# A planner that counts TensorE's changes of tiling mode and takes attention products in groups

## The chip, the cores and the metric

The kernel runs on one core of a Trainium2 chip. Its time is device microseconds of one execution; the median of three is 494.1 us (493.23 to 494.2). One more execution was profiled, and took 493.1 us. The engines are TensorE (PE in the profile, its weight loads PEld), VectorE (DVE), ScalarE (ACT), GpSimd (POOL) and SyncE (SP, which issues most DMAs).

## The reference

Linear attention with a decaying state, then a Fourier mixing over tokens and channels, a normalization and a feed-forward network (FFN), for 4 batches of 768 tokens, 8 heads of 48 and 384 channels:

```python
for t in range(S):
    state = alpha[:, :, t, :, None] * state + np.einsum('bhd,bhe->bhde', k[:, :, t], v[:, :, t])
    y[:, :, t] = np.einsum('bhd,bhde->bhe', q[:, :, t], state)
...
X = np.fft.fft(x, axis=1)
X = np.fft.fft(X, axis=2)
mixed = np.real(X).astype(np.float32)
u = x + mixed
mu = np.mean(u, axis=-1, keepdims=True)
var = np.mean((u - mu) ** 2, axis=-1, keepdims=True)
un = (u - mu) / np.sqrt(var + 1e-06)
ch = np.maximum(un @ w_ch1, 0.0) @ w_ch2
return (u + ch).astype(np.float32)
```

## The kernel before

**Work.** The recurrence is computed in chunks of 64 and 128 tokens. Two heads are handled together as a *pair* (4 pairs in a batch), one in rows 0 to 47, the other in rows 64 to 111. The stages of a pair (`attn_stages`, L750) are: scans of the decay on DVE (`s1` to `s3`), five transposes of keys (`s4`, tile `kt`), twelve *products* of keys and queries (`s5`: 48 rows deep, 128 x 128 out, copied by ACT to tiles of `w` or `x` and masked by POOL), ten *updates* (`s6`: keys times values, `vn`, 48 x 48 out into one PSUM tile) that DVE scales and chains to the states `tt`, and `s7`: for each half of the tokens 12 *values* (masked products times values, 64 columns wide) and 4 or 6 *state* matmuls (queries times `tt`, 112 rows, 64 columns) into one PSUM tile, which ACT copies to `y`. When the four pairs are done, *mixing* (`mix_stages`, L953) folds the sequence on DVE into `z` and takes 24 DFT matmuls with constants (`cst`) over tokens, then 12 over channels and two of one row; `norm_stages` (L1076) normalizes and takes nine transposes for each of the two token blocks, whose results are the FFN's input `x`. The FFN (`ffn_stages`, L1129) splits weights and inputs in a high and a low part: 432 matmuls a batch of 128 x 128 weights by 384 columns.

**PSUM.** Eight banks: three tiles `a` (attention, mixing and norms), two `f1` and three `f2` (FFN). Up to the first FFN matmul the attention may use all of them. The profile calls both of the FFN's `f`.

**Classes.** TensorE takes a matmul with over 64 rows and over 64 weight columns on the whole array (FFN, transposes, most of the DFT), one with at most 64 rows in a mode of short rows (products), one with at most 64 columns in a mode of narrow columns (updates, values, state); dummies and the one-row DFT matmuls have at most 32 columns, a mode of their own.

**Order.** Each operation is recorded with a key, and a `Plan` simulates all engines with estimated durations (`simulate`, L395). It writes the program in the order that this gives; all recorded operations therefore stand on L562 in the profile. Of the operations that an engine could start first, the one with the lowest key goes first. FFN matmuls (`fill`) of batch b have keys from b*1000+500, attention of batch b+1 from b*1000+420 (`KA`, `K1`), its mixing with the norm of the first token block b*1000+410 (`KM`), and the norm of batch b's own second block b*1000-595 (`KN`, so 405 for batch 1). So FFN work of one batch fills TensorE while attention and mixing of the next one come ready. The waiting rule (L460 to L464): right after an FFN matmul, operations that are ready, are no fill and have a key of 400 (`TOGETHER`) or more are kept back while fill is ready, until they sum up to 1.3 us (`ENOUGH`) or the first of them has waited 1.0 us (`PATIENCE`). Batch 0's attention has negative keys and runs alone, with dummies on `zero` (L1343 and L1345) put by count into TensorE's simulated gaps. `FX` lets the plan put some weight operations on DVE or POOL.

Of the kernel before, what the change touches and what calls it, by code (L numbers as in the profile page):

```python
# [33 lines left out]
GRP = 64  # L34
# [34 lines left out]
LONG = 3.0  # L69
FIRST = 2.8  # L70
NEAR = 3.0
TOGETHER = 400.0
ENOUGH = 1.3
PATIENCE = 1.0
LATE = 4.0
FAR = 12.0
SHORT = 20.0
# [120 lines left out]
class Plan:  # L198
# [39 lines left out]
    def add(self, engines, name, args, kwargs):  # L238
        engine = engines[0]
        fns = {e: self.method(e, name) for e in engines}  # L240
        if self.direct:
            return fns[engine](*[real(a) for a in args], **{k: real(x) for k, x in kwargs.items()})
        op = Op(engines, fns, args, kwargs, self.key)
        n = len(self.ops)
        self.ops.append(op)
        named = [("out" if i == 0 and "out" not in kwargs else i, a) for i, a in enumerate(args)] + list(kwargs.items())
        op.free, op.fill = 1, self.fill
        op.crit = CRIT[0] < self.key < CRIT[1] and not self.low
        op.bytes = None
        for k, a in named:  # L250
            if isinstance(a, Rows):
                a = a.view
            if isinstance(a, View):
                self.touch(n, op, a, k in ("out", "accum_out"))
                if k == "out":
                    op.free = self.region(a)[4]
                if k == 2:
                    op.moving = a
        op.name, op.loose = name, self.loose
        named = dict((str(k), a) for k, a in named)  # L260
        op.durs = {e: self.duration(op, named, e) for e in engines}
        op.port = self.port(op, named) if engine in ("DVE", "POOL") else None
        if engine == "SP" and isinstance(named["out"], View) and not self.loose:
            if self.chain is not None and self.chain not in op.deps:
                op.behind = self.chain
                op.deps.add(self.chain)
            self.chain = n
        if "dma" in name:
            op.wire = self.wire(named)

    def hold(self, view):

# [122 lines left out]
    def simulate(self, ghost=False, guess=None):  # L395
# [43 lines left out]
            due = coming[e][0][0] + shift if coming[e] else 1e9  # L439
            return t + op.durs[e] > due + HOLD[e] and t < due + GRACE  # L440

        placed, filled = 0, False
        while placed < len(ops):
            placed += 1
            best, spare = None, None
            for e, cand in wait.items():
# [11 lines left out]
                            continue  # L458
                    times.append((t, max(now, t), n))
                if e == "PE" and filled:  # L460
                    due = [x for x in times if x[0] <= now and not ops[x[2]].fill and ops[x[2]].key >= TOGETHER]
                    if due and any(x[0] <= now and ops[x[2]].fill for x in times):
                        if sum(ops[x[2]].durs[e] for x in due) < ENOUGH and now - min(x[0] for x in due) < PATIENCE:
                            times = [x for x in times if x not in due]  # L464
                if not times:
                    continue
# [1 line left out]
                for some, held_back in ((free, False), (times, True)):  # L468
                    if not some or (held_back and free):
                        continue  # L470
                    first = min(x[1] for x in some)
                    key, n, t = min((ops[n].key, n, max(t, now)) for t, late, n in some if late <= first + WINDOW[e])
                    if held_back:
                        if spare is None or t < spare[0]:
                            spare = (t, n, e)
                    elif best is None or t < best[0]:
                        best = (t, n, e)
# [7 lines left out]
            op.engine, op.dur = engine, op.durs[engine]  # L485
            if engine == "PE":
                filled = op.fill
            if guess and op.crit:
                for x in coming.values():
                    while x and done[x[0][1]]:  # L490
                        x.pop(0)
                shift = t - guess[n][0]
# [87 lines left out]
def gla_mix_ffn(ctx: ExitStack, tc: tile.TileContext, alpha, chunked, kq, pairkq, v, w1, w2, consts, rowtab, out):  # L580
# [169 lines left out]
    def attn_stages(b, hp, i, mixed, last):  # L750
# [115 lines left out]
                    G.affine_select(out=xs, in_=xs, pattern=[[0, 3], [1, P]], compare_op=ALU.is_ge, fill=0.0, base=0, channel_multiplier=-1)  # L866

        def s6():
            pu = psa()
            for a in range(NT - 1):  # L870
                for hd, r0 in enumerate((0, GRP)):
                    T.matmul(
                        pu[r0 : r0 + D, a * D : (a + 1) * D], e["kt"][:, a, r0 : r0 + D],
                        loaded["vn", pair][:, (2 * a + hd) * D : (2 * a + hd + 1) * D], start=True, stop=True,
                    )
            mt = e["mt"]
            for hd, r0 in enumerate((0, GRP)):
                r = slice(r0, r0 + D)
# [9 lines left out]
        def s7():  # L888
            X = e["X"]
            ytiles = mixed()[0]  # L890
            for h2 in range(2):
                py = psa()
                for c in range(3):
                    cc = 3 * h2 + c
                    cs = slice(cc * P, (cc + 1) * P)
# [7 lines left out]
                    if cc:  # L903
                        for lo in (0, GRP):
                            yo = py[lo : lo + GRP, o : o + 2 * GRP].rearrange("p (h e) -> p h e", h=2)[:, :, 0:D]
                            T.matmul(yo, e["A"][0:CW, cs.start + lo : cs.start + lo + GRP], tt[0:CW, cc - 1], start=False, stop=True)
                yo = py[:, 0 : 6 * GRP].rearrange("p (a h e) -> p a h e", a=3, h=2)[:, :, :, 0:D]
                FL["ev"].copy(ytiles[h2][:, :, hp * 2 * D : (hp + 1) * 2 * D].rearrange("p a (h e) -> p a h e", h=2), yo)

# [608 lines left out]
```

## Time and profile before

| | |
|---|---|
| median of three runs | 494.1 us |
| profiled execution | 493.1 us, span 491.4 us |
| granted TensorE clock | 0.999 of full speed |
| FFN matmuls | 1728, mean 341 to 342 ns to their modelled ends |
| values `a<-vn,w` | 576 records, mean 224 ns |
| state `a<-tt,w` | 288 records, mean 259 ns |
| products `a<-w,al` | 306 records, mean 289 ns |
| first FFN matmul | 70.47 us |

A group's duration in the table reaches to the modelled end of a matmul, and matmuls overlap; starts that follow each other tell the pace. The page names instructions by line, engine, operation, and out<-in without buffer numbers.

### The profile page before, as it was taken

What the parts mean: (1) busy time and instruction counts of PE and PEld (TensorE: products, weight loads), DVE (VectorE), ACT (ScalarE), POOL (GpSimd) and SP (SyncE); (2) the same over time, 40 slices, a digit from 0 to 9 for tenths busy, and PEclk for the clock granted to TensorE, in tenths of its full rate; (3) what the DMA queues carried; (4) which work ended last, traced back from release to release, by engine and by line L of the source; (5) the groups of instructions that cost most, each with busy time, mean ns of one, the idle gap of its engine ahead of it and who ended that gap; (6) DMA issues with size and microseconds to landing.
All of it is one profiled execution on the core that took longest, in us unless ns stands there. A gap on an engine that the chain in (4) does not pass through costs nothing.

```text
span 491.4 us, 10884 instructions
## 1 busy us (share of the span) xinstructions
PE 481.6 (98%) x4532; PEld 449.1 (91%) x4532; DVE 312.3 (64%) x693; ACT 182.9 (37%) x382; POOL 59.7 (12%) x86
## 2 busy tenths in 40 slices
PE   7999999999999999999999999999999999999995
PEld 6888989888889998888899999888999999999995
DVE  8878999886769997726599914736559314113112
ACT  3487487446762235443222314333112213111110
POOL 0321263101112000211020000122020000000000
PEclk9999999999999999999999999999999999999999
DMA  8869323327506022250140201110120001001001
GB/s 302 309 182 403 104 68 110 112 60 251 172 10 202 2 80 65 57 214 26 61 143 9 73 16 50 46 31 1 49 72 28 1 0 49 0 1 48 1 0 55
DMA packets 17687, 42.58 MB, mean 87 GB/s; under 512 B 2688, under 2 KB 8000, under 8 KB 17632
## 3 DMA queue, kind: packets, MB, share of 16 engines
q1 hardware_dynamic: 16576, 39.39, 23.8%
q0 software_dynamic: 768, 2.36, 1.8%
q8 instruction: 38, 0.62, 0.5%
q14 instruction: 17, 0.14, 0.1%
q10 hardware_dynamic: 288, 0.07, 0.1%
HBM read 31.97 MB, written 7.08 MB: 79 GB/s over the span
## 4 chain that ended last, share of the span: by engine, by line
PE 97%; DVE 2%; ACT 0%; ACTq 0%; issue 0%
PE f L562 67%; PE a L562 24%; PE a L1343 3%; PE f L1345 2%; PE f L1343 2%; DVE y L562 1%; DVE al L562 0%; ACT L562 0%; DVE st L562 0%; ACTq L562 0%; DVE x L562 0%; DVE mv L562 0%; ACT zero L562 0%; DVE w L562 0%; DVE back L562 0%
## 5 line engine op out<-in xcount | busy, mean ns | idle before, releaser
L562 PE MATMUL f<-x,wt 128*128 128x384 f32 x864 | 175.1, 342 | 0.7 <-ACT x L562 0.4
L562 PE MATMUL f<-wt,h 128*128 128x384 f32 x864 | 174.4, 341 | 0.0
L562 PEld LDWEIGHTS f<-x,wt 128*128 128x128 f32 x864 | 150.3, 188 | 3.4 <-DVE x L562 0.6
L562 PEld LDWEIGHTS f<-wt,h 128*128 128x128 f32 x864 | 149.7, 188 | 2.7 <-issue 0.2
L562 DVE SCALAR_TENSOR_TENSOR h<-f,h 128x384 fp32r<-128x384 f32 x96 | 53.2, 555 | 115.6 <-ACT h L234 115.0
L234 ACT ACTIVATE h<-f 128x384 fp32r<-128x384 f32 x96 | 47.1, 492 | 167.7 <-PE f L562 167.3
L562 POOL TENSOR_SCALAR_AFFINE_SELECT w<-w 128x384 f32<-128x384 f32 x48 | 25.2, 547 | 204.4 <-ACT w L562 204.4
L562 ACT COPY w<-a 128x384 f32<-128x384 f32 (+4 forms) x59 | 26.0, 482 | 41.9 <-PE a L562 41.9
L562 PE MATMUL a<-vn,w 128*64 128x64 f32 x576 | 27.4, 224 | 0.0
L562 DVE TENSOR_TENSOR tt<-a,w 48x240 f32<-48x240 f32 x30 | 12.1, 405 | 23.2 <-PE a L562 22.9
L562 PEld LDWEIGHTS a<-vn,w 128*64 128x64 f32 x576 | 23.6, 137 | 3.2 <-issue 3.0
L562 PE MATMUL a<-tt,w 112*64 112x96 f32 x288 | 26.3, 259 | 0.0
L562 DVE SCALAR_TENSOR_TENSOR y<-f,r,y 128x384 f32<-128x384 f32 x30 | 17.2, 613 | 13.7 <-PE f L562 13.7
L562 PEld LDWEIGHTS a<-w,al 48*128 48x128 f32 x306 | 19.7, 187 | 5.6 <-issue 4.3
L562 PE MATMUL a<-w,al 48*128 48x128 f32 x306 | 24.7, 289 | 0.0
L562 ACT COPY y<-a 128x288 f32<-128x288 f32 x29 | 11.6, 399 | 29.8 <-PE a L562 29.7
L562 DVE TENSOR_TENSOR y<-y,a 128x192 f32<-128x192 f32 (+6 forms) x66 | 20.6, 361 | 1.7 <-PE a L562 1.6
L562 DVE TENSOR_TENSOR_SCAN w<-al,d 128x768 f32<-128x768 f32 (+1 forms) x13 | 21.2, 1630 | 0.7 <-PE a L562 0.6
L562 DVE TENSOR_TENSOR_SCAN al<-al,back 128x768 f32<-128x768 f32 (+1 forms) x13 | 21.2, 1632 | 0.0
L562 DVE SCALAR_TENSOR_TENSOR tt<-tt,w 112x96 f32<-112x96 f32 x64 | 20.5, 321 | 1.0
L562 PEld LDWEIGHTS a<-tt,w 112*64 112x64 f32 x288 | 14.8, 136 | 6.0 <-issue 2.3
L562 DVE TENSOR_TENSOR z<-f 128x288 f32<-128x288 f32 (+3 forms) x40 | 19.7, 532 | 0.0
(128 smaller groups left out, 529.6 us busy)
## 6 DMA issues: line engine op xcount, KB each, us to landing
kq<-in_kq_dram SPq DMA_DIRECT2D x10, 768.0 KB, 6.7
wt<-in_w_dram SPq DMA_DIRECT2D x8, 768.0 KB, 6.0
out_dram<-y SPq DMA_DIRECT2D x24, 192.0 KB, 1.9
al<-in_chunked_dram SPq DMA_DIRECT2D x11, 392.0 KB, 4.7
vn<-in_v_dram SPq DMA_DIRECT2D x14, 296.0 KB, 4.1
wt<-in_w_dram SPq DMA_DIRECT2D x8, 384.0 KB, 6.2
scr<-y SPq DMA_DIRECT2D x4, 576.0 KB, 4.3
w<-w SPq DMA_DIRECT2D x28, 48.3 KB, 2.1
```

Of the source, the lines that this page charges most:

```text
L234: return lambda out, x: e.activation(out, x, AF.Relu)
L562: op.ins = op.fns[op.engine](*[real(a) for a in op.args], **{k: real(x) for k, x in op.kwargs.items()})
L1343: short = lambda *b: nc.tensor.matmul(bank(*b)[0:32, 480:512], zero.real(), zero.real(), start=True, stop=True)
L1345: long = lambda *b: nc.tensor.matmul(bank(*b)[0:32, 384:512], zero.real(), wide.real(), start=True, stop=True)
```

## The change

Two constants give a price to a change of mode in the plan: 0.09 us, and 0.19 us where the next operation is fill. Each recorded matmul gets a mode from its rows and columns (transposes count as mode 0). After an operation that is no fill, TensorE's candidates that can start no later than the first and have the same mode as the last one are taken first, if they are no fill, have a key of 400 or more and need no new tile. `together(n)` makes operations from number n on a group: the first gets the dependences on earlier operations and the tiles of all, the others depend on it. It is called for the ten updates of a pair and for each half's values and state, from batch 1 on. In the waiting rule, only operations whose key is at 420 or more in its thousand are kept back, so mixing (410) and the norms (410 and 405) are not; the two limits become tuples of equal values. No matmul, copy or DMA is added or taken away, but for the dummies.

```diff
+SWITCH = 0.09
+RETURN = 0.19
-ENOUGH = 1.3
-PATIENCE = 1.0
+ENOUGH = (1.3, 1.3, 1.3)
+PATIENCE = (1.0, 1.0, 1.0)
...
+        op.mode = 0
+        if engine == "PE" and name == "matmul":
+            (k0, k1), (m0, m1) = (self.region(dict(named)[x])[0:2] for x in (1, "out"))
+            op.mode = (1 if k1 - k0 <= GRP else 0) + (2 if m1 - m0 <= GRP else 0)
...
+    def together(self, n):
+
+        if not self.direct:
+            group = range(n, len(self.ops))
+            for m in group:
+                self.ops[n].deps |= {d for d in self.ops[m].deps if d < n}
+                if m > n:
+                    self.ops[m].deps.add(n)
+                for slot in self.ops[m].slots:
+                    if slot not in self.ops[n].slots:
+                        self.ops[n].slots.append(slot)
+                        slot.uses += 1
...
                 if e == "PE" and filled:
-                    due = [x for x in times if x[0] <= now and not ops[x[2]].fill and ops[x[2]].key >= TOGETHER]
+                    due = [x for x in times if x[0] <= now and not ops[x[2]].fill and ops[x[2]].key % 1000.0 >= KA and ops[x[2]].key >= TOGETHER]
                     if due and any(x[0] <= now and ops[x[2]].fill for x in times):
-                        if sum(ops[x[2]].durs[e] for x in due) < ENOUGH and now - min(x[0] for x in due) < PATIENCE:
+                        k = min(int(ops[x[2]].key // 1000) for x in due)
+                        if sum(ops[x[2]].durs[e] for x in due) < ENOUGH[k] and now - min(x[0] for x in due) < PATIENCE[k]:
...
                     first = min(x[1] for x in some)
+                    if e == "PE" and not filled:
+                        like = [x for x in some if x[1] <= first and ops[x[2]].mode == mode and not ops[x[2]].fill and ops[x[2]].key >= TOGETHER and all(s.cell is not None or not s.tag for s in ops[x[2]].slots)]
+                        some = like or some
...
             if engine == "PE":
                 filled = op.fill
+                if op.mode != mode:
+                    mode, op.dur = op.mode, op.dur + (RETURN if op.fill else SWITCH)
...
         def s6():
-            pu = psa()
+            pu, n = psa(), len(plan.ops)
...
+            if b:
+                plan.together(n)
...
-                py = psa()
+                py, n = psa(), len(plan.ops)
...
+                if b:
+                    plan.together(n)
```

TensorE, the values and state of batch 2's second pair (209.68 us before). `vn` are values, `w` with them a masked product, `tt` the state, `cst,al` a transpose of the next pair's keys. Before:

```order
L562 MATMUL a_379_2675<-vn_271_1982,w_3_367_2605 64x64 x8
L562 MATMUL a_379_2675<-tt_130,w_0_308_2236 64x2x48 x2
L562 MATMUL a_379_2675<-vn_271_1982,w_3_367_2605 64x64 x4
L562 MATMUL a_380_2693<-vn_271_1982,w_4_373_2641 64x64 x3
L562 MATMUL a_379_2675<-tt_130,w_0_308_2236 64x2x48 x2
L562 MATMUL a_380_2693<-vn_271_1982,w_4_373_2641 64x64
L562 MATMUL a_381_2701<-cst,al_275_1995 128x112
L562 MATMUL a_380_2693<-tt_130,w_0_308_2236 64x2x48 x2
L562 MATMUL a_380_2693<-vn_271_1982,w_4_373_2641 64x64 x4
L562 MATMUL a_381_2701<-cst,al_275_1995 128x112 x2
L562 MATMUL a_382_2712<-cst,al_275_1995 128x112 x2
L562 MATMUL a_380_2693<-tt_130,w_0_308_2236 64x2x48 x2
```

and of the change:

```order
L587 MATMUL f_1_336_2413<-wt_0_158_1181,h_377_2664 128x384
L587 MATMUL a_383_2704<-vn_271_1966,w_3_367_2600 64x64 x8
L587 MATMUL a_383_2704<-tt_130,w_0_318_2291 64x2x48 x2
L587 MATMUL a_383_2704<-vn_271_1966,w_3_367_2600 64x64 x4
L587 MATMUL a_383_2704<-tt_130,w_0_318_2291 64x2x48 x2
L587 MATMUL a_385_2724<-vn_271_1966,w_4_373_2627 64x64 x4
L587 MATMUL a_385_2724<-tt_130,w_0_318_2291 64x2x48 x2
L587 MATMUL a_385_2724<-vn_271_1966,w_4_373_2627 64x64 x4
L587 MATMUL a_385_2724<-tt_130,w_0_318_2291 64x2x48 x2
L587 MATMUL a_385_2724<-vn_271_1966,w_4_373_2627 64x64 x4
L587 MATMUL a_385_2724<-tt_130,w_0_318_2291 64x2x48 x2
```

The five transposes have moved ahead of an FFN run (they stand eight rows earlier), and each half's values are followed by their state without anything between.

TensorE, the change from the FFN of batch 0 to that of batch 1 (183.2 us before). `cst,f` and `cst,h` are the norms' transposes, `wt,h` FFN matmuls of batch 0, and those with `x_32` ahead of batch 1. Before:

```order
L562 MATMUL f_1_286_2101<-wt_0_273_1989,h_317_2295 128x384 x3
L562 MATMUL f_2_288_2108<-wt_0_273_1989,h_317_2295 128x384
L562 MATMUL a_323_2337<-cst,f_314_2276 128x128 x2
L562 MATMUL f_2_288_2108<-wt_0_273_1989,h_317_2295 128x384 x2
L562 MATMUL f_0_289_2113<-wt_0_273_1989,h_317_2295 128x384 x3
L562 MATMUL a_319_2304<-cst,f_314_2276 128x128
L562 MATMUL a_321_2312<-cst,f_314_2276 128x128
L562 MATMUL a_323_2337<-cst,f_314_2276 128x128
L562 MATMUL f_0_326_2360<-x_324_2354,wt_0_106_779 128x384 x2
L562 MATMUL f_1_328_2366<-x_324_2354,wt_0_106_779 128x384
L562 MATMUL f_0_326_2360<-x_325_2356,wt_0_106_779 128x384 x2
L562 MATMUL f_0_326_2360<-x_327_2362,wt_0_107_792 128x384 x2
```

and of the change:

```order
L587 MATMUL a_328_2355<-cst,h_325_2337 128x128
L587 MATMUL a_329_2357<-cst,h_325_2337 128x128
L587 MATMUL f_1_287_2102<-wt_0_270_1957,h_324_2330 128x384
L587 MATMUL a_327_2352<-cst,h_326_2347 128x128
L587 MATMUL a_328_2355<-cst,h_326_2347 128x128
L587 MATMUL a_329_2357<-cst,h_326_2347 128x128
L587 MATMUL f_2_289_2110<-wt_0_270_1957,h_324_2330 128x384
L587 MATMUL f_0_290_2114<-wt_0_270_1957,h_324_2330 128x384
L587 MATMUL f_0_331_2375<-x_319_2293,wt_0_104_736 128x384 x2
L587 MATMUL f_0_331_2375<-x_321_2303,wt_0_104_736 128x384 x2
L587 MATMUL f_0_331_2375<-x_322_2308,wt_0_108_790 128x384 x2
L587 MATMUL f_0_331_2375<-x_319_2293,wt_0_104_736 128x384
```

All 18 transposes of batch 1's norms now stand before its first FFN matmul, with FFN work of batch 0 between them; before, nine of them came behind it.

DVE, the start (11 us before). The operations on 768 elements of `w` with `d` and of `al` with `back` are the scans, `tt_129` the first pair's state. Before:

```order
L562 SCALAR_TENSOR_TENSOR w_2_3_68<-al_36_101,d_131 128x768
L562 RECIPROCAL back<-w_2_3_68 128x6
L562 RECIPROCAL rec<-w_2_3_68 128x6
L562 TENSOR_TENSOR w_2_3_68<-w_2_3_68 128x5
L562 TENSOR_TENSOR tt_129<-f_0_48_113,w_0_1_66 48x5x48 x2
L562 SCALAR_TENSOR_TENSOR al_36_101<-al_36_101,back 128x768
L562 SCALAR_TENSOR_TENSOR tt_129<-tt_129,w_0_1_66 112x96
L562 TENSOR_TENSOR w_2_3_68<-w_2_3_68,rec 128x6x64
L562 SCALAR_TENSOR_TENSOR tt_129<-tt_129,w_0_1_66 112x96
```

and of the change:

```order
L587 SCALAR_TENSOR_TENSOR w_2_3_68<-al_36_101,d_131 128x768
L587 RECIPROCAL back<-w_2_3_68 128x6
L587 RECIPROCAL rec<-w_2_3_68 128x6
L587 TENSOR_TENSOR w_2_3_68<-w_2_3_68 128x5
L587 SCALAR_TENSOR_TENSOR al_36_101<-al_36_101,back 128x768
L587 TENSOR_TENSOR tt_129<-f_0_48_113,w_0_1_66 48x5x48 x2
L587 TENSOR_TENSOR w_2_3_68<-w_2_3_68,rec 128x6x64
L587 SCALAR_TENSOR_TENSOR tt_129<-tt_129,w_0_1_66 112x96
L587 TENSOR_TENSOR al_36_101<-kq_40_105,al_36_101 128x768
```

The scan of `al_36` has moved ahead of the two products that wait for the first updates.

More of the change, by code (lines that the diff above doesn't have):

```diff
@@ L440, in blocks @@
             return t + op.durs[e] > due + HOLD[e] and t < due + GRACE
-        placed, filled = 0, False
+        placed, filled, mode = 0, False, 0
         while placed < len(ops):
```

## The prediction

> **What bounds the kernel now.** I read the page first, then the chain of waits, then the waits, and last the timeline of TensorE in narrow windows.
>
> ```profile
> span 491.4 us, 10884 instructions
> ...
> PE 481.6 (98%) x4532; PEld 449.1 (91%) x4532; DVE 312.3 (64%) x693; ACT 182.9 (37%) x382; POOL 59.7 (12%) x86
> ...
> PE 97%; DVE 2%; ACT 0%; ACTq 0%; issue 0%
> ```
>
> The profiled execution took 493.1 us, 1.7 us of it outside the span; the median of the three runs is 494.1 us, 1.0 us more. TensorE (PE) carries 97% of the chain that ended last. Its busy share alone would prove little, because ends of matmuls are modelled. What counts is how far the starts of successive matmuls lie apart.
>
> ```profile
> 146.72 19.75 PE f L562 x112
> 166.47 8.71 PE a L562 x68
> ```
>
> These rows of the chain (start, duration, what) show 112 FFN matmuls in a row in 19.75 us: **0.176 us each**, the pace with nothing in between. The timeline of TensorE in the second pair of batch 2 shows what happens around attention work; its columns are start, time to the modelled end, operation, names, shape of the weights, count of records. An FFN matmul and a transpose are one record each, every other matmul two.
>
> ```profile
> 188.30 1.15 PE L562 MATMUL a<-cst,h 128*128 128x128 f32 x9
> 189.20 1.30 PE L562 MATMUL f<-x,wt 128*128 128x384 f32 x6
> ...
> 204.69 1.49 PE L562 MATMUL f<-wt,h 128*128 128x384 f32 x7
> 206.02 0.69 PE L562 MATMUL f<-x,wt 128*128 128x384 f32 x3
> 206.63 0.94 PE L562 MATMUL a<-w,al 48*128 48x128 f32 x12
> 206.85 0.50 PE L562 MATMUL a<-w,al 48*128 48x128 f32 x6
> 206.96 0.50 PE L562 MATMUL a<-w,al 48*128 48x128 f32 x6
> 207.50 0.66 PE L562 MATMUL a<-vn,kt 128*48 128x48 f32 x20
> 207.85 0.30 PE L562 MATMUL a<-vn,kt 128*48 128x48 f32 x6
> 208.09 1.31 PE L562 MATMUL f<-x,wt 128*128 128x384 f32 x6
> 209.24 0.51 PE L562 MATMUL f<-wt,h 128*128 128x384 f32 x2
> 209.68 0.69 PE L562 MATMUL a<-vn,w 128*64 128x64 f32 x16
> 210.19 0.34 PE L562 MATMUL a<-tt,w 112*64 112x96 f32 x4
> 210.36 0.57 PE L562 MATMUL a<-vn,w 128*64 128x64 f32 x13
> ...
> 212.69 0.40 PE L562 MATMUL a<-vn,w 128*64 128x64 f32 x8
> 212.92 0.34 PE L562 MATMUL a<-tt,w 112*64 112x96 f32 x4
> 213.19 1.13 PE L562 MATMUL f<-wt,h 128*128 128x384 f32 x5
> ```
>
> (The rows of 206.85, 206.96 and 207.85 come from windows that begin inside a run.) Ten FFN matmuls between two attention pieces take 204.69 to 206.63, 1.94 us, where 10 x 0.176 is 1.76: 0.18 too much. Six products (48*128) take 0.87; inside the run they start 0.11 apart, so 0.66 was due: 0.21 too much. Ten updates (128*48) take 0.59; the first seven took 0.35, 0.05 each, so 0.50 was due: 0.09 too much. That round, FFN to products to updates to FFN, has three changes of the weights' shape class (full, short rows, narrow columns) and 0.48 us that no matmul explains: **0.16 us a change**.
>
> The stretch from 209.68 to 213.19 gives the price again: 24 values (0.23 us for four at 212.69, 0.058 each), ten state matmuls (0.17 for two at 210.19, 0.085 each) and five transposes (about 0.10, from 0.90 for nine at 188.30) make 1.39 + 0.85 + 0.50 = 2.74 us of the 3.51. Of the 0.77 left, the way in (0.51 at 209.68 for eight values, 0.05 over pace) and the way out (0.27 at 212.92 for two state matmuls, 0.10 over) take 0.15. Four changes between values, transposes and state take 0.62: again 0.16 each. Values and state have one class; between them the pace shows nothing.
>
> ```profile
> PEld a L562 <- issue: 11.1, 44, 0.3
> ```
>
> This row of the waits, TensorE's weight loads from 70.5 us to the last matmul, says it in another way: 44 times a load stood for about 0.25 us with no other engine to wait for.
>
> **The change, part by part.** *Fewer class changes.* Counted over the two built orders from the first FFN matmul on (70.47 us before) to the last one, consecutive matmuls change class 144 times before and 98 times after; by batch stage 49, 46, 45 and 4 before, 37, 29, 28 and 4 after. The work is the same: 1728 FFN, 192 products, 384 values, 160 state, 160 updates. Transposes stand amid values and state less often (25 changes before, 2 after), and FFN work no longer splits a half (from FFN to state 18 and none, from values to FFN 12 and none); the other kinds rise by 7. 46 x 0.16 = **7.4 us less**. Two changes from products to values and one from transposes to values are in no row of before; between products-to-updates and the dearest run above they cost 0.1 to 0.2 each, and I take 0.16. For the whole count the bounds are 46 x 0.09 = 4.1 (the least excess above) and 46 x 0.21 = 9.7 us; I take 0.16 since both stretches give it.
>
> *Groups.* The new dependences exist in the plan alone: on the chip a matmul waits for what it reads. But in TensorE's order a half's values now stand behind the state they are grouped with, and their evacuations behind them, then the mixing. What covers that delay is FFN work between the last attention matmul and the first mixing one: 112, 47 and 41 matmuls before, 102, 52 and 39 after in the three stages, at 0.176 still 18.0, 9.2 and 6.9 us. Without that cover a group's delay, at most the 3.5 us of the stretch above, would show. I cost it at nothing.
>
> *Mixing and norms exempt.* Their matmuls are of the full class, like the FFN's, so a piece alone costs no change. What it may move is the only place after 70.5 us where TensorE ran dry:
>
> ```profile
> 185.53 1.48 PE L562 MATMUL f<-x,wt 128*128 128x384 f32 x7 [0.36 <-ACT x L562]
> ...
> 187.32 1.14 PE L562 MATMUL f<-x,wt 128*128 128x384 f32 x5 [0.31 <-DVE x L562]
> ...
> 181.00:188.00 7.00, 6.33 (x38) 5.43 (x36) 6.96 (x17) 3.45 (x8) 0.00 (x0) 1.00 0.20 72
> ```
>
> The last row has busy time of PE, PEld, DVE and so on in 181 to 188 us: DVE is full (6.96 of 7.00) with additions and norms of batch 1, while TensorE has 0.67 us of nothing because the FFN of batch 0 has run out. Behind the last DFT matmul of batch 1, 17 FFN matmuls of batch 0 are left before and 61 after, 44 x 0.176 = 7.7 us more cover. I take **0.7 us less**; bounds 0 and, with the stretched FFN run at 185.53 (seven matmuls in 1.79 us, 0.56 over pace), 1.2.
>
> *The start, up to 70.5 us.* Class changes there hardly fall, 79 to 77, and are not what ends last.
>
> ```profile
> 0.00:70.50 70.50, 67.20 (x1108) 60.00 (x1108) 61.69 (x134) 42.17 (x83) 19.49 (x27) 1.00 0.64 226
> 70.50:150.00 79.50, 79.50 (x775) 71.48 (x774) 64.33 (x127) 47.91 (x92) 14.03 (x19) 1.00 0.41 131
> ...
> 14.13 0.82 DVE L562 TENSOR_TENSOR tt<-f,w 48x240 f32<-48x240 f32 x2 [1.31 <-PE f L562]
> 14.99 1.76 DVE L562 TENSOR_TENSOR_SCAN al<-al,back 128x768 f32<-128x768 f32 x1
> ...
> 46.51 9.74 PE L1345 MATMUL f<-zero 128*32 128x128 f32 x86
> 56.94 0.95 DVE L562 TENSOR_TENSOR wt<-wt,wt 128x768 fp32r<-128x768 f32 x1
> ```
>
> DVE works 61.69 of 70.50 us and mostly bounds; TensorE fills its gaps with dummies on zeros. In the new order DVE scans first and takes `tt` after it, so the 1.31 us wait at 12.8 is filled, and 36 long dummies stand where there were 43 (9.74/43 = 0.23 each, 1.6 us fewer). Against it, POOL hands one weight subtraction to DVE, 0.95 us by the last row. It comes behind the first FFN matmul's inputs, where DVE has 15 us free (64.33 of 79.50), and those hide it. I take **0.5 us less**, from bounds of 1.6 less and 0.95 more, nearer the middle as DVE's work ahead of the first FFN matmul is the same but for one operation of half a microsecond.
>
> *New waits.* Packed groups leave less room before an evacuation is needed: I add 0.5 us, about what TensorE lost at 181 to 188, from bounds of 0 and the slow rival below.
>
> **Sum.** -7.4 - 0.7 - 0.5 + 0.5 = -8.1 us. 493.1 - 8.1 = 485.0 for an execution like the profiled one, and 1.0 more for the median: **486.0 us**.
>
> **Rivals.** *A change is cheaper than its stretch.* If the excess is mostly weight loads that stay bare in a group as well, only 0.09 a change goes: 4.1 us and nothing else, 490.0. For it: at 208.09 eight FFN matmuls take 1.59 us, 0.18 too much, shared by two changes, so each FFN side is 0.09. Against it: both stretches sum to 0.16 when all sides are counted.
>
> ```profile
> L562 PEld LDWEIGHTS f<-wt,h 128*128 128x128 f32 x864 | 149.7, 188 | 2.7 <-issue 0.2
> ```
>
> Loads of 0.188 us fit a pace of 0.176, so inside a class a load hides beneath the matmul before it. The Trainium skill (TensorE: Matmul & The Clock Gate, Part 3, "What overlaps and what doesn't") holds that a load overlaps matmuls in flight only where its row group differs; FFN weights all use the full rows, so by that rule loads would be bare already and a change would cost just its drain, which is this rival's case. By that rule, the trace disagrees: a bare load alone would exceed the pace.
>
> *Evacuations set the pace: slower.* A half's values now stand together, and ACT must copy each PSUM tile out before one of the three tiles `a` comes free.
>
> ```profile
> L562 ACT COPY y<-a 128x288 f32<-128x288 f32 x29 | 11.6, 399 | 29.8 <-PE a L562 29.7
> ```
>
> A copy takes 0.40 us. There are 12 grouped pairs with three groups each. If each of the 36 stood bare by 0.23 us, the 8.1 us would be gone: no change. With the whole copy bare it is 36 x 0.40 = 14.4 us, and the time 494.1 - 8.1 + 14.4 = 500.4. For it: three tiles only. Against it: ACT waited 29.7 us for TensorE before these copies, not the reverse, and seven or more FFN matmuls (1.2 us) usually separate attention pieces. The Trainium skill (TensorEngine Tiling (Array Packing), "PSUM Bottleneck") warns that tiling speeds up TensorE but not the evacuation; no row of before shows TensorE waiting for one.
>
> *All bounds fall well.* 46 x 0.21 is 9.7 us, with 0.7 and half of 1.6 in the start 11.2: 483.
>
> *The plan does not do on the chip what it counts.* The saved changes are handed back where DVE is full (6.96 of 7.00 us): at most the gain of the first stage, 12 x 0.16 = 1.9 us, so this alone gives 488, inside the forecast's own spread of 484.5 to 488.5.
>
> **Chances.** Forecast 0.62; cheaper changes 0.14 (490.0); all bounds 0.12 (483); evacuations up to the 0.23 us point, no change, 0.05; beyond it 0.07 (about 500). The range takes in forecast and the two beside it: 482.5 to 491.0. Faster by over 0.2% (about what a measurement of this kernel can tell from no change) 0.88, within 0.2% 0.05, slower 0.07.
>
> **What would show it.** In the profile after, the row of loads waiting on "issue" should fall from 44 times to about 30; FFN matmuls should keep 0.176 us; values and state of a pair should run from start to end without a gap at 0.058 and 0.085 us; TensorE should have no idle time at the change from batch 0 to 1; the first FFN matmul should start near 70 us. Wrong it would be if `PE a <- ACT` waits appear (evacuations), if the excess in runs that remain grows over 0.16 us (the price was not per change), or if the first FFN matmul comes after 71.5 us.

## The result, and the profile after

The median is 486.05 us (485.96 to 486.44, four executions) against 493.67 us for the kernel before beside it: a ratio of **0.985, 95% interval [0.983, 0.987]**, 7.6 us less. The profiled execution took 485.96 us with a span of 484.3 us, 7.1 us less than before.

The page of the changed kernel: the span, the engines' busy time, and the shares of the chain that ended last.

```profile
span 484.3 us, 10874 instructions
...
PE 473.7 (98%) x4526; PEld 447.9 (92%) x4526; DVE 312.6 (65%) x695; ACT 181.2 (37%) x381; POOL 63.6 (13%) x85
...
PE 95%; ACT 1%; DMA 1%; SPq 0%; POOL 0%; DVE 0%; issue 0%; ACTq 0%
```

TensorE bounds it as before, and 98% busy tells as little as it did. Four views carry the reading. The first is the timeline of TensorE at the second pair of batch 2, the place where the prediction took its price (start, time to the modelled end, operation, weights, records).

```profile
207.95 0.65 PE L587 MATMUL a<-cst,al 112*128 112x112 f32 x5
208.36 1.82 PE L587 MATMUL f<-x,wt 128*128 128x384 f32 x9
210.03 0.33 PE L587 MATMUL f<-wt,h 128*128 128x384 f32 x1
210.29 0.69 PE L587 MATMUL a<-vn,w 128*64 128x64 f32 x16
...
212.40 0.34 PE L587 MATMUL a<-tt,w 112*64 112x96 f32 x4
212.67 0.96 PE L587 MATMUL f<-wt,h 128*128 128x384 f32 x4
```

The 24 values and ten state matmuls of the pair run from 210.29 to 212.67, 2.38 us, with nothing between them; before they took 3.51 us with five transposes among them. The transposes now stand between FFN matmuls and take 0.41 (207.95 to 208.36); the nine FFN matmuls behind them take 1.67, where 9 x 0.176 is 1.58, and that 0.09 is theirs too. So the five still cost 0.50, and 3.51 - 2.38 - 0.50 is 0.63 us saved here, 0.16 for each of four changes fewer. Next the pace, from the chain of work that ended last (start, duration, what):

```profile
143.61 18.04 PE f L587 x102
```

and the waits of TensorE's weight loads from 70 us to the end (us in total, times, longest):

```profile
PEld a L587 <- issue: 8.2, 32, 0.4
```

FFN keeps 0.177 us a matmul (18.04 / 102), and the row on "issue" fell from 44 times and 11.1 us to 32 and 8.2. The third view is a window at the change from batch 0 to batch 1 (busy time of PE, PEld, DVE, ACT and POOL):

```profile
181.00:188.00 7.00, 7.00 (x45) 6.92 (x44) 6.74 (x12) 4.06 (x9) 0.00 (x0) 1.00 0.26 80
```

and TensorE's timeline at its end, where the FFN of batch 1 begins:

```profile
184.26 0.49 PE L587 MATMUL a<-cst,h 128*128 128x128 f32 x3
184.51 0.60 PE L587 MATMUL f<-wt,h 128*128 128x384 f32 x2
184.94 3.34 PE L587 MATMUL f<-x,wt 128*128 128x384 f32 x18
```

TensorE no longer runs dry there (7.00 of 7.00, 6.33 before). The fourth view is the timeline again, of the first FFN matmuls of all; its first row is from before, where that run begins at 70.47:

```profile
73.83 1.77 PE L562 MATMUL f<-wt,h 128*128 128x384 f32 x9
...
68.99 3.43 PE L587 MATMUL f<-x,wt 128*128 128x384 f32 x18
72.58 1.14 PE L587 MATMUL f<-wt,h 128*128 128x384 f32 x5 [0.17 <-ACT h L236]
```

and ACT's at the same time:

```profile
70.56 1.28 ACT L587 ACT_TABLE_LOAD   x1
...
72.06 0.47 ACT L236 ACTIVATE h<-f 128x384 fp32r<-128x384 f32 x1
```

FFN begins at 68.99 instead of 70.47, 1.48 us earlier. Its first 18 matmuls take 3.59 us; before they took 3.36 (70.47 to 73.83). The first matmul on `h` waits 0.17 us for ACT, which loads a table for 1.28 us ahead of it. This small stall is new.

So far everything points one way. What doesn't is the length of the stages, from the first FFN matmul of a batch to that of the next (the last, to the last matmul):

| batch | 0 | 1 | 2 | 3 |
|---|---|---|---|---|
| before, us | 115.07 | 111.98 | 111.24 | 76.49 |
| after, us | 115.95 | 108.59 | 108.41 | 76.06 |
| class changes, cut at the same marks | 53 to 39 | 44 to 29 | 45 to 28 | unchanged |

Batches 1 and 2 fall by about 0.16 us a change (2.4 and 2.7 of 3.4 and 2.8). Batch 0's stage has 14 changes fewer, lost the first of the two dry places, and is 0.9 us *longer*. That 0.9 is the mark and not the kernel: by the trace's records the four stages held 18, 21, 18 and 6 transposes of the norms before and hold 27, 18, 18 and none after, so nine of them, 0.9 us at 0.10 each, were moved into this stage. (The six that left batch 3's stage are its 0.43 less, with a wait of 0.17 against them.) Like for like the stage is as long as before, where 14 changes (2.2) and the dry place (0.6) should have made it 2.8 us shorter. The products that run in it, those of batch 1, show why. First a usual set of six (two heads, three chunks; TensorE's timeline around 214 us), then one from batch 1, with ACT's copy of the transposes ahead of it:

```profile
214.25 0.94 PE L587 MATMUL a<-w,al 48*128 48x128 f32 x12
215.12 1.85 PE L587 MATMUL f<-x,wt 128*128 128x384 f32 x9
...
96.50 0.69 ACT L587 COPY kt<-a 128x336 f32<-128x336 f32 x2
99.25 0.34 PE L587 MATMUL a<-tt,w 112*64 112x96 f32 x4
99.51 0.93 PE L587 MATMUL a<-w,al 48*128 48x128 f32 x6
100.38 1.50 PE L587 MATMUL f<-x,wt 128*128 128x384 f32 x7
101.81 0.93 PE L587 MATMUL a<-w,al 48*128 48x128 f32 x6
102.67 0.62 PE L587 MATMUL f<-wt,h 128*128 128x384 f32 x2
```

Six products whose heads alternate take 0.87 us (214.25 to 215.12; two records each). In the lower rows three products of *one* head stand alone, FFN follows, then the other head's three: each trio takes 0.87 and 0.86 as well. Half the work takes the same time. By the trace's records, two to a product, a head's records stand 0.11 us apart in both cases, but for 0.21 behind the first; in the usual set the other head's stand 0.01 behind them (214.255 and 214.262), so both heads run side by side, and a trio runs alone.

It is so in three of batch 1's eight sets, because the plan gave the set one PSUM tile `a` at that point where it takes two. The transposes did not hold the other: ACT had copied them out 2.3 us before (at 97.19, by the row above), and 2.3 and 0.6 us before in the other two places. The kernel's text gives a reason that no run tests by itself: a tile is given out of the recorded order only while one more stays free (`KEEP`); the second half's values, recorded earlier and now a group that isn't ready, have not taken theirs; and the set's first product asks for two tiles at once, the other head's for one.

3 x 0.86 = 2.6 us: the 48 products of this stage took 6.95 us before and 9.52 now. Of neighbouring products on the same rows there are 12 after the change and 4 before, those in the start.

### The profile page after: what moved, and what is told of

It reads as the page before. It is cut to its first block, busy times and chain, and to the rows that moved or that the text cites. A ratio compares the mean times of both kernels' runs of the same rounds, so it can differ in the third digit from the quotient of the medians.

```text
span 484.3 us, 10874 instructions
## 1 busy us (share of the span) xinstructions
PE 473.7 (98%) x4526; PEld 447.9 (92%) x4526; DVE 312.6 (65%) x695; ACT 181.2 (37%) x381; POOL 63.6 (13%) x85
## 4 chain that ended last, share of the span: by engine, by line
PE 95%; ACT 1%; DMA 1%; SPq 0%; POOL 0%; DVE 0%; issue 0%; ACTq 0%
PE f L587 67%; PE a L587 24%; PE f L1374 2%; PE f L1372 1%; DMA al<-in_chunked_dram 1%; PE a L1372 1%; SPq L587 0%; ACT c L587 0%; POOL x L587 0%; DVE y L587 0%; ACT x L587 0%; ACT h L236 0%; ACT L587 0%; ACT f L587 0%; ACT kt L587 0%
## 5 line engine op out<-in xcount | busy, mean ns | idle before, releaser
L587 POOL TENSOR_SCALAR_AFFINE_SELECT w<-w 128x384 f32<-128x384 f32 x48 | 28.7, 619 | 196.8 <-ACT w L587 196.8
L587 PE MATMUL a<-w,al 48*128 48x128 f32 x306 | 27.6, 289 | 0.0
L587 PEld LDWEIGHTS a<-w,al 48*128 48x128 f32 x306 | 21.9, 187 | 5.8 <-issue 3.8
L587 PE MATMUL a<-tt,w 112*64 112x96 f32 x288 | 24.6, 248 | 0.0
L587 DVE SCALAR_TENSOR_TENSOR y<-f,r,y 128x384 f32<-128x384 f32 x30 | 17.1, 613 | 10.2 <-PE f L587 10.1
L587 POOL DMA_INDIRECT y<-scr,rows x12 | 14.6, 1213 | 55.4 <-DMA scr<-y 38.7
L587 DVE TENSOR_TENSOR y<-y,a 128x192 f32<-128x192 f32 (+5 forms) x66 | 20.7, 362 | 1.6 <-PE a L587 1.6
```

The costliest lines, as they stand in the source:

```text
L587: op.ins = op.fns[op.engine](*[real(a) for a in op.args], **{k: real(x) for k, x in op.kwargs.items()})
```

## Experiments

The change stands at 486.05 us; the kernel before, beside these runs, at 493.52 (first four), 493.17 (the next four), 493.22 and 493.15 (the last three). Intervals are those of the ratio to it. As it moves by 0.5 us from group to group, differences to the change of less than that say nothing.

**The groups taken out** (`e1_no_groups`): the price of a change against its rival.

```diff
-            if b:
-                plan.together(n)
...
-                if b:
-                    plan.together(n)
```

> The change without its groups (updates, values and state are planned one by one again); the price of a mode change, the preference for the same mode and the exemption stay. The built order has 133 class changes from the first FFN matmul on, against 98 with groups, and no two products on the same rows behind one another, against 12. Theory (each change costs 0.16 us, each product behind one on the same rows 0.11 us): 35 x 0.16 - 12 x 0.11 = 4.3 us more than the change, about 490.4 us. Rival (groups delay evacuations and cost what they save): no difference, 486 us. Rival (a change costs 0.09): 35 x 0.09 - 1.3 = 1.8 more, 487.9 us. The first FFN matmul starts at 69.0 us, as with groups.

Measured: 490.0 us, 0.994 [0.992, 0.996], 3.95 more than the change. The order has 133 changes instead of 98, and no two neighbouring products of one head. 35 x 0.16 = 5.6 less the 2.6 of the products is 3.0; with 0.09 a change it would be 0.6. The stages tell it more cleanly. Batches 1 and 2, with the same transposes and without a split set in either kernel, last 110.41 and 110.50 us against 108.59 and 108.41: 3.9 us for 25 changes, 0.156 each. Of the 0.9 us that isn't accounted for, 0.5 lies in batch 0's stage (115.52 against 115.95, where 10 changes more and no split set make 1.0 less), and 0.4 between medians and profiled executions (3.54 to the last matmul). The waits of TensorE's loads from 70 us on:

```profile
PEld a L587 <- issue: 8.1, 32, 0.3
PEld a L587 <- POOL w L587: 2.2, 9, 0.3
```

The "issue" row is the same as the changed kernel's, though this order has 35 changes more. The prediction wanted to read it as a count of changes. It counts ways from FFN into other work (36 for 36 lone probes below), and part of them stand under another releaser's name.

**Prices and preference for the same mode taken out** (`e2_no_mode`):

```diff
-SWITCH = 0.09
-RETURN = 0.19
+SWITCH = 0.0
+RETURN = 0.0
-                    if e == "PE" and not filled:
+                    if e == "PE" and False:
```

> The change without the price of a mode change and without the preference for the same mode; groups and exemption stay. The order has 106 class changes from the first FFN matmul on (98), 12 products on the same rows (12), and 43 long dummies in the start as before (36). Theory: 8 x 0.16 = 1.3 us for changes, and if the price is what moved the start, the first FFN matmul is back at 70.5 us and that adds 1.5 us: 488.8 us. Rival (the start moved for another reason, such as the groups): first FFN matmul at 69.0 and 487.3 us.

Measured: 487.72 us, 0.989 [0.987, 0.991], 1.7 more than the change. The order has 106 changes (8 x 0.16 = 1.3), and 43 long dummies stand in the start again; the first FFN matmul is at 70.14, 1.15 later, and doesn't meet the table load. The two make 2.4, more than came, so what the prices do through the count of dummies in the start counts about as much as the changes they save. The theory's 488.8 was too high, the rival's 487.3 nearer.

**The waiting rule as before** (`e3_mix_waits`): mixing and norms kept back again.

```diff
-... and ops[x[2]].key % 1000.0 >= KA and ops[x[2]].key >= TOGETHER]
+... and ops[x[2]].key >= TOGETHER]
-                        k = min(int(ops[x[2]].key // 1000) for x in due)
+                        k = min(2, min(int(ops[x[2]].key // 1000) for x in due))
```

> The change with mixing and norms kept back by the waiting rule again; price, preference and groups stay. The order has 102 class changes from the first FFN matmul on (98) and 16 products on the same rows (12). Theory: 4 x 0.16 + 4 x 0.11 = 1.1 us more, 487.1 us, and TensorE has gaps again between the FFN of batch 0 and that of batch 1 (0.7 us): 487.8 us. Rival (the exemption does nothing that counts): 486 us, no gaps there.

Measured: 487.3 us, 0.988 [0.987, 0.990], 1.25 more than the change. The theory's number is met, its reason hardly: the dry places do not come back. TensorE's timeline there:

```profile
186.59 1.15 PE L587 MATMUL a<-cst,h 128*128 128x128 f32 x9
...
188.25 0.51 PE L587 MATMUL a<-cst,al 112*128 112x112 f32 x3 [0.16 <-DVE x L587]
```

There is one wait of 0.16 us. The rest fits 102 changes (4 x 0.16 = 0.6) and 16 same-row neighbours instead of 12, which is one more split set (0.86). In `e1_no_groups` and `e2_no_mode` TensorE is busy through 181 to 190 us too, so the place stays full whichever of the three parts is left out, and which of them fills it stays open.

**Products as a group** (`e4_pairs`): the split sets repaired. From batch 1 on, a set's products form a group, and a pair's first transpose takes its target `kt` before it starts, so that it can't sit on PSUM.

```diff
                 for a in range(a0, a1):
                     T.transpose(...)
+                    if a == 0 and b:
+                        plan.hold(kt)
...
-                pc = [psa() for _ in range(2)]
+                pc, n = [psa() for _ in range(2)], len(plan.ops)
...
+                if b:
+                    plan.together(n)
```

> The change with the six products of a half as a group too, and the transposes of a pair taking their place in PSUM only when the tile that they are copied to is free. The order has 93 class changes from the first FFN matmul on (98), and no products on the same rows behind one another (12). Theory: 5 x 0.16 + 12 x 0.11 = 2.1 us less than the change, and the split runs of three products are gone: 483.7 us. Rival (products of one head are slow for their distance from other work, not for their rows, or the groups now delay the copies): 486 us or more.

Measured: **483.56 us**, 0.981 [0.979, 0.983], 2.5 less than the change. Batch 0's stage is 112.99 us long (115.95 in the change), and the set that was split at 99.51 takes what the others take, 106.98 to 107.85:

```profile
106.98 0.94 PE L587 MATMUL a<-w,al 48*128 48x128 f32 x12
107.85 1.31 PE L587 MATMUL f<-wt,h 128*128 128x384 f32 x6
```

There are no same-row neighbours left and 93 changes; the first FFN matmul is at 69.34, 0.35 later. 2.6 + 0.8 - 0.35 = 3.05 were due by that count, 2.5 came (2.59 to the last matmul). The two edits were not run apart.

**All sets with one head after the other** (`e5_same_rows`): the suspected cost, doubled and more, on the changed kernel.

```diff
-                for c in range(3):
-                    cs = slice(...)
-                    for hd, r in ((0, slice(0, D)), (1, slice(GRP, CW))):
+                for hd, r in ((0, slice(0, D)), (1, slice(GRP, CW))):
+                    for c in range(3):
+                        cs = slice(...)
```

> The change with the six products of a half in another order: three of one head, then three of the other, in place of one of each in turn. The same work; the order has 124 products behind one on the same rows against 12, 104 class changes from the first FFN matmul on against 98. Theory (a product behind one on the same rows starts 0.22 us after it, on the other rows 0.11 us): 96 such products behind the first FFN matmul are 84 more than now, 84 x 0.11 + 6 x 0.16 = 10.2 us more, 496 us, and inside a run of three the starts lie 0.22 us apart everywhere. Rival (the runs of three were slow because each was cut off by FFN work, so two class changes fell on three products): 487 us, starts 0.11 us apart.

Measured: 494.43 us (ten executions), 1.003 [1.001, 1.004], 8.4 more than the change. A change of two loops that adds no instruction gives back all that the change gained. The size was expected at 10.2; six in a run cost less than two trios:

```profile
92.62 1.26 PE L587 MATMUL a<-w,al 48*128 48x128 f32 x12
93.81 0.66 PE L587 MATMUL a<-vn,kt 128*48 128x48 f32 x20
```

1.19 us for six in this order, 0.87 alternating, 0.86 for three alone. By the trace's records the first head's run from 92.62 to 93.28 and the second's from 92.95 to 93.61, in each the products 0.33 and then 0.22 apart, as in a trio. So "0.22 apart on the same rows" held. What the sum lacked is that the second head starts 0.33 us behind the first and runs beside it: four same-row neighbours in a set cost 0.32 us, not 4 x 0.11.

**The price by itself** (`p1_spread`, `p2_bunch`, `p3_full`): 36 probes, small matmuls of 32 columns of zeros with a weight tile of 64 columns, in the last 216 FFN matmuls of batch 3, where nothing else runs. In `p1_spread` each stands alone, which makes 170 changes in the program; in `p2_bunch` they stand at one place, 100 changes; `p3_full` is `p1_spread` with weights of 128 columns, FFN's class, 98 changes.

```diff
+    def probe(times):
+        if "to" not in probing:
+            probing["to"] = psa()
+        for _ in range(times):
+            T.matmul(probing["to"][0:GRP, 0:32], ident[:, 0:GRP], zero, start=True, stop=True)
+            plan.ops[-1].deps.add(len(plan.ops) - 2)
...
# p2_bunch: if f == f0: probe(36)
# p3_full: T.matmul(probing["to"][:, 0:32], ident, zero, start=True, stop=True)
```

> The change with 36 extra matmuls of narrow columns (64 weight columns, 32 moving columns, on zeros) in the last 216 FFN matmuls, one ahead of each three that finish a token block, so that each stands alone: 72 class changes more, 170. Their results are not used. Theory: against the kernel with 36 extra matmuls on the whole array at the same places, 72 x 0.16 = 11.5 us more. Rival (0.09 us a change): 6.5 us. Rival (0.20 us, as the plan's two constants of 0.09 and 0.19 make 0.14 each): 10.1 us for 0.14.

> The change with the same 36 narrow matmuls all at one place of the last FFN: 2 class changes more, 100. Theory: they cost their pace alone, about 0.05 us each, 1.8 us, and 0.3 us for two changes: 488.2 us. The kernel with them spread is then 70 x 0.16 = 11.2 us slower than this one. Rival (a narrow matmul is itself dear, changes are not): this one costs as much as the spread one.

> The change with 36 extra matmuls on the whole array (128 weight columns, 32 moving columns, on zeros) at the places of the spread narrow ones: no class change more, 98. Theory: about 0.1 us each for a load of 128 columns and a short matmul, 3.6 us: 489.7 us, and FFN matmuls beside them keep 0.176 us. Rival (any foreign matmul amid FFN work breaks its pace, whatever its class): as much as the spread narrow ones, 497 us or more.

Measured: 502.09 us, 1.018 [1.016, 1.021]; 490.42, 0.994 [0.992, 0.996]; 493.94 (ten executions), 1.0015 [1.000, 1.003]. TensorE's timeline of `p1_spread`:

```profile
455.33 0.30 PE L587 MATMUL a<-zero,cst 128*64 128x32 f32 x2
455.56 0.80 PE L587 MATMUL f<-wt,h 128*128 128x384 f32 x3
456.29 0.30 PE L587 MATMUL a<-zero,cst 128*64 128x32 f32 x2
```

of `p2_bunch`:

```profile
445.62 4.38 PE L587 MATMUL a<-zero,cst 128*64 128x32 f32 x72
449.93 2.38 PE L587 MATMUL f<-wt,h 128*128 128x384 f32 x12
```

and of `p3_full`:

```profile
452.69 0.30 PE L587 MATMUL a<-zero,cst 128*128 128x32 f32 x2
452.83 0.77 PE L587 MATMUL f<-wt,h 128*128 128x384 f32 x3
453.44 0.30 PE L587 MATMUL a<-zero,cst 128*128 128x32 f32 x2
```

A probe in the bunch takes 4.31 / 36 = 0.12 us. A round of one probe alone and three FFN matmuls takes 0.96 (455.33 to 456.29), less 0.12 and 3 x 0.176 that is 0.31 for two changes. The two medians give 11.67 / 70 = **0.167 us a change**, the two spans (499.8 and 489.4) 0.15. That is the mean price, by work that shares nothing with attention.

Against `p3_full` 11.5 us were expected and 8.15 came. The third probe was meant to show a probe without a change, and is poorer at that: its round is 0.75, so a probe takes 0.22, not the expected 0.1 and 0.10 more than one of the bunch. With that 36 x 0.10 put back it is 11.75 us, 0.163 for each of 72 changes. Is the 0.22 a price for standing alone among FFN matmuls? Hardly, by an estimate: a transpose, one record with weights of the same 128 columns, takes 0.10 in a run (0.90 for nine at 188.30 before), so a probe of two records would take 0.20 anyway. No run puts 36 of these at one place.

The probes also show what the row on "issue" counts (`p1_spread` from 400 us on), one wait for each probe, though each makes two changes:

```profile
PEld a L587 <- issue: 9.0, 36, 0.3
```

**Dearer changes in the plan** (`e6_price`, on `e4_pairs`): both prices at 0.2, `SWITCH = 0.2` and `RETURN = 0.2`.

> The kernel with the products grouped, and the plan's two prices set to 0.2 us each (0.09 and 0.19). The order has 92 class changes from the first FFN matmul on (93), 18 short dummies fewer in the start, no products on the same rows. Theory (0.16 us a change, the start set by DVE): 0.2 us less than the kernel with the products grouped, 483.4 us. Rival (the start follows the dummies): up to 18 x 0.06 = 1.1 us less, 482.5 us.

Measured: ten executions that scatter, five from 485.82 to 486.34 us, the profiled one 486.01 among them, four from 487.89 to 496.23, and one of 1576.32, which no run explains; the median of all is 487.11, the ratio 0.988 [0.985, 0.991]. The five lie 2.4 us above `e4_pairs`; 483.4 was expected, and missed. Behind the start it is like `e4_pairs`; the loss lies ahead of it, as TensorE's timeline shows (the last number is idle time and what ended it):

```profile
62.42 0.98 PE L587 MATMUL a<-cst,x 96*128 96x192 f32 x4 [0.41 <-DVE y L587]
...
71.55 0.61 PE L587 MATMUL f<-x,wt 128*128 128x384 f32 x2
```

The first FFN matmul comes 2.2 us later than in `e4_pairs`. The DFT begins 0.57 of it later (55.18 against 54.61); behind it TensorE waits for DVE's `y` three times, 0.91 us in all, and dummies fill more. A price in the plan moves batch 0's order as well, where there is hardly a change to save.

**Seven long dummies more** (`e7_dummies`, on the change): does DVE set the start, or do the dummies?

```diff
-... * int((t - t0) / DUMMY[kind]))
+... * (int((t - t0) / DUMMY[kind]) + 7 * (kind == 1)))
```

> The change with seven more long dummies ahead of the DFT of batch 0, 43 as before the change; nothing else differs. Theory (the dummies stand in front of the first DFT matmul, which has its input by then): the DFT starts 7 x 0.22 = 1.5 us later, the first FFN matmul at 70.5 us instead of 69.0, 487.5 us. Rival (DVE's work ahead of the first FFN matmul, 1.1 us earlier than before, sets the start): the first FFN matmul stays at 69.0 to 69.5 us, 486.0 to 486.5 us.

Measured: 487.74 us, 0.990 [0.988, 0.992], 1.7 more than the change, as expected. TensorE's timeline:

```profile
46.11 9.74 PE L1374 MATMUL f<-zero 128*32 128x128 f32 x86
55.78 3.89 PE L587 MATMUL f<-cst,z 128*97 128x65 f32 x36
...
70.42 0.79 PE L587 MATMUL f<-x,wt 128*128 128x384 f32 x3
```

The DFT follows its dummies at once, and FFN begins at 70.42, as in the kernel before: seven matmuls on zeros held up the first FFN matmul.

**Five long dummies fewer** (`e8_fewer`, on `e4_pairs`): the same line with `- 5 * (kind == 1)`. Is there more to be had?

> The kernel with the products grouped, and five long dummies fewer ahead of the DFT of batch 0 (31 in place of 36); nothing else differs. Theory (the dummies still stand in front of the first DFT matmul): it starts 5 x 0.22 = 1.1 us earlier or as soon as DVE has its input, and the time falls by 0.5 to 1.1 us, 482.5 to 483.1 us. Rival (its input from DVE comes last by now): no difference, 483.6 us, with TensorE idle ahead of the first DFT matmul.

Measured: 483.2 us, 0.980 [0.978, 0.981], not clearly different from the 0.981 [0.979, 0.983] of `e4_pairs`. TensorE's timeline:

```profile
46.70 7.07 PE L1378 MATMUL f<-zero 128*32 128x128 f32 x62
54.55 3.86 PE L587 MATMUL f<-cst,z 128*97 128x65 f32 x36 [0.78 <-PE f L1378]
```

and DVE's:

```profile
53.58 2.87 DVE L587 TENSOR_TENSOR z<-f 128x6 int32<-128x6 int32 x5
```

TensorE is idle for 0.78 us ahead of the DFT. The releaser named is the last dummy, long done; what comes in just then is `z`, which DVE writes from 53.58 on, 0.97 us ahead of the DFT. In `e4_pairs` it is 1.25 (53.36 and 54.61), so with 36 dummies the start is within 0.3 us of DVE's own pace.

## Why the prediction was right, point by point

The predicted 486.0 us stands beside 486.05. So close a meeting was luck, for the sum was not that good. By its terms, in us to the last matmul of the profiled executions:

| term | predicted | found |
|---|---|---|
| 46 changes fewer | -7.4 | -7.4 (the count at 0.16; at 0.15 to 0.167 by the probes -6.9 to -7.7) |
| dry place at 181 to 188 us | -0.7 | -1.2 |
| start | -0.5 | -1.48 |
| new waits | +0.5 | +0.3 |
| products of one head alone | not seen | +2.6 |
| sum | -8.1 | -7.2 |

The last matmul starts 7.25 us earlier (485.25 to 478.00), the span is 7.1 shorter. The 0.9 us by which the sum was too low were made good by the 1.0 us that was added for the median: the changed kernel's median lies 0.1 above its profiled execution, not 1.0.

*Fewer class changes.* Right, price and count. The stretch of batch 2's second pair gave 0.63 for four changes, `e1_no_groups` 3.9 for 25, the probes 0.15 to 0.167 in work of their own, and batches 1 and 2 fell as the count says. The rival of 0.09 (490.0 us) falls with them, and with `e1_no_groups`. The Trainium skill (TensorEngine Tiling (Array Packing), "Key Properties") says that a change of the tiling mode, not of the tile alone, drains TensorE; the trace agrees, with 0.31 us a round around a lone probe and 0.12 for one among its like.

*Groups at nothing.* This step failed. The prediction looked for the price of a delay on ACT's side and on the cover, and cover there was. What a group does is to wait for its PSUM tile until all of it is ready, and while the second half's values waited so, the plan left a set of products one tile. The set was split by head, and three products on one head's rows take as long as six on two. A count of classes is blind to it: 14 changes fewer brought 2.2 us in batch 0's stage and the split cost 2.6. The experiments that undo it (`e4_pairs`, 2.5 us) and that widen it (`e5_same_rows`, 8.4 us) show it in the time as well as in the rows; `e1_no_groups`, without groups, has no split set. Only the plan's reason is read from its text and not tested.

It was in reach. The Trainium skill (TensorE: Matmul & The Clock Gate, Part 3, "What overlaps and what doesn't") ties the overlap of a weight load to another row group, and the prediction set that rule aside because FFN, with full rows, keeps 0.176 us with loads of 0.188. For FFN the trace still disagrees with it. For short rows the trace agrees that the row group decides, 0.87 us for six that alternate and 0.86 for three that don't, but not that loads on the same rows stay bare: a trio's loads of 0.187 us stand 0.11 apart.

*Exemption and the dry place.* The place closed, for 1.2 us: before, three transposes at about 0.1 took 0.91 us there (184.62 to 185.53, 0.6 lost), and seven FFN matmuls 1.79 (0.56 lost).

```profile
184.62 0.55 PE L562 MATMUL a<-cst,f 128*128 128x128 f32 x3
```

That is the upper bound, 1.2, rather than 0.7. The exemption is worth 1.25 us in all, yet without it the place stays closed but for 0.16, as it does without the groups or the prices.

*The start.* The mechanism was named and its size was wrong. "DVE mostly bounds" was read from 61.69 of 70.50 us busy, an average over a stage. The rows at the first DFT matmul, TensorE's and DVE's, tell more, two from before and two of the change:

```profile
56.18 3.89 PE L562 MATMUL f<-cst,z 128*97 128x65 f32 x36
54.10 2.93 DVE L562 TENSOR_TENSOR z<-f 128x6 int32<-128x6 int32 x6
...
54.36 3.89 PE L587 MATMUL f<-cst,z 128*97 128x65 f32 x36
52.97 2.93 DVE L587 TENSOR_TENSOR z<-f 128x6 int32<-128x6 int32 x6
```

The DFT began 2.08 us after DVE's first `z` before and 1.39 after, where 0.97 is enough (`e8_fewer`). So dummies held it, 43 and then 36, and the bound of 1.6 less, seven dummies at 0.23, was the measured case, 1.48; `e7_dummies` shows it by putting them back. DVE had its part: its `z` comes 1.13 us earlier. With `z` at 54.10 the DFT could have begun at 55.07 at the earliest, an estimate from that 0.97, and 0.7 of the 1.48 would have been lost.

*New waits.* Two came, 0.3 us in all, and not where they were looked for: matmuls on `h` wait for ACT, 0.17 us at 72.58 behind its table load and 0.17 at 405.53. (An idle spell of 0.13 behind DVE's `y` at 170.90 comes on top.) No wait of `PE a` for ACT is found from 60 us on, so the slow rival, evacuations laid bare, didn't occur.

*The rival of what the plan doesn't count* came nearest in kind. It put the loss at 1.9 us in the first stage, where DVE is full. The loss was there, at 2.6 us, but of TensorE's own making.

## What to carry to other kernels

Count two things where small matmuls mix with large ones: each change of the array's mode (0.16 us here), and each pair of short-row neighbours on the same rows; and where some small matmuls are planned as groups, group those as well that take PSUM tiles from the same few (2.5 us here). A busy share of an engine doesn't say what ends a wait at one place: read the row just ahead of the work that waits, and test whether filler work put by a plan holds up the real work. Where a forecast meets the time, take its terms apart all the same: here a cost of 2.6 us that the sum did not have was covered by 1.7 us from terms that came out better and 1.0 us added for a median that did not need it.

## What the runs showed of the hardware

- Products of 48 rows by 128 columns: six take 0.87 us when heads alternate, 1.19 with three of one head and then three of the other, and three of one head alone take 0.86, ways in and out included. The two heads, in rows 0 to 47 and 64 to 111, run side by side.
- A matmul of 32 columns takes 0.12 us in a run with a weight tile of 128 x 64, and 0.22 between FFN matmuls with one of 128 x 128, where the mode doesn't change.
- Values and state matmuls that follow each other in one mode lose nothing: 24 and ten in 2.38 us, where their paces of 0.058 and 0.085 give 2.24, and the way in and out takes the rest.
